# A new hand-written order of the first chunk's work, some of it on other engines, and softmax sums stored two words apart

## The chip, the cores and the metric

The kernel runs on one core of a Trainium2 chip. The metric is device time in microseconds (us) of one execution. The median of three runs of the kernel before is 609.96 us (609.53 to 610.3).

## The reference

```python
def _attn_ref(q, k, v):                      # q, k, v: 4 x 8 x 768 x 64
    block, window = (32, 16)
    k_sum = k.reshape(B, H, nb, block, D).max(axis=3)
    v_sum = v.reshape(B, H, nb, block, D).mean(axis=3)
    scores_l = scale * np.matmul(q, k.transpose(0, 1, 3, 2))
    mask_l = np.abs(pos[:, None] - pos[None, :]) < window
    scores_s = scale * np.einsum('bhsd,bhnd->bhsn', q, k_sum) + np.log(block)
    scores_all = np.concatenate([np.where(mask_l, scores_l, -1e9), scores_s], axis=-1)
    a = np.exp(scores_all - np.max(scores_all, axis=-1, keepdims=True))
    a = a / (np.sum(a, axis=-1, keepdims=True) + 1e-09)
    return np.matmul(a, np.concatenate([v, v_sum], axis=2))

def _moe_ref(x, w_in, w_out):                # 3072 x 512, 512 x 2048, 2048 x 512
    h = x @ w_in
    g = np.where(h > 0.0, h, np.exp(np.minimum(h, 0.0)) - 1.0)
    return g @ w_out
```

Each query sees the 31 keys around it and 24 block summaries of its head. The eight heads' outputs, side by side, are the rows x of a two-layer network with an ELU between the layers.

## The kernel before

The 3072 rows are six chunks of 512. A chunk takes 16 steps f of the network: twelve matmuls of the first layer into a PSUM tile `h`, the ELU of `h` on ScalarE and VectorE, and twelve matmuls of the second layer, which add into four PSUM tiles `o`. Twelve and not four, because every operand is split into a rounded high part and a remainder (`xh` and `xl`, `gh` and `gl`, a high and a low half of `w`) and three of the four products are formed. The weights come as 64-bit words and are made into fp32 on the chip during the first chunk: a conversion is GpSimd's or ScalarE's low bits (words X, Y), ScalarE's exponent (M), two VectorE operations (S), the high half (H) and the remainder (L). There are 32 conversions; number j alternates between the layers: 0 is step 0 of the first layer, 1 is step 1 of the first, 2 is step 0 of the second, and so on.

Attention runs ahead of the network. The first 512 queries are done by `first_units` at the very start, for four pairs of heads p, each with two halves h of the even and odd head. Later groups g of queries go between the network's steps.

From the start to the end of chunk 0 nothing sets the order but the string `FIRST`: each word is a piece of work and an engine may be its last number. Words are issued in the order of the string, and each engine runs its own instructions in that order (`tc.manual_schedule` for all five engines); semaphores are waited for where data needs it. The words that matter below:

- `kq`, `ve`, `vo`, `w`: loads on SyncE's queue of keys and queries, of value windows (`ve.0` to `ve.3`, `vo`) and of weight j.
- `max` (VectorE): block maxima of a pair's keys, L344. `sl`, `ss` (TensorE): window and summary scores. `low` (VectorE, L176, four instructions and four accumulator reads): masks and row maxima. `exp` (ScalarE, L184): exponentials, their sums written to a tile `zs`. `z` (VectorE): adds 1e-9 to a pair's eight sums (L189) and takes reciprocals (L190). `norm` (L193): multiplies a half by them, on GpSimd (last number 0) or VectorE (1). `tr`, `ptc`: transposes on TensorE and the copy from PSUM. `sums`, `spr`, `mv`: block means of the values on TensorE, spread by copies. `val` (TensorE): outputs of a pair. `xh`, `xl`: the split into `xs`.
- `first` and `L1h`, `L1l`: first-layer products of a step, with the high and low weights. `E`, `gap`, `larger`: the ELU as exp, relu(1 - e) on ScalarE and a maximum on VectorE (L689); `ts`, `stt` do the last two on VectorE instead. `G`, `gl`: the split of g. `L2a`, `L2b`, `L2c`: second-layer products.
- `gsc`, `glow`, `ge`, `gz`, `gn`, `gtr`, `gpc`, `gb`, `gval`, `gxh`, `gxl`: the same pieces for the later groups; `gb` transposes 32 x 32 blocks on VectorE (L606).
- `idle`, `warm`: matmuls of zeros, whose result nobody reads.

PSUM ties engines together: `h` has two buffers, so that `L1h` of a step waits for the `larger` (or the group's `gxl`) of two users earlier, and the scores of a group use the two banks in which S works. After the string comes the loop over the other 80 steps, which does not change.

Of the kernel before, what the change touches and what calls it, by code (L numbers as in the profile page):

```python
# [40 lines left out]
FIRST = """
    kq.2 sl.0 kq.3 max.0 ss.0 low.0.1 ve.2 exp.0.1 max.1 low.0.0 exp.0.0 sl.1 idle.1.196 ss.1 low.1.0 exp.1.0 max.2
    low.1.1 z.0 norm.0.0.0 sl.2 idle.1.220 ss.2 sl.3 idle.1.360 ve.1 exp.1.1 low.2.1 exp.2.1 max.3 z.1 ss.3 low.2.0
    exp.2.0 w.0 norm.0.1.0 norm.1.1.0 low.3.1 low.3.0 norm.1.0.0 exp.3.0 tr.0.0.1 tr.0.1.0 warm.1.144 z.2 tr.1.0.3
    ve.0 sums.0 sums.1 ve.3 vo exp.3.1 X.0 norm.2.0.0 ptc.0.1.0 sums.2 ptc.0.0.0 norm.2.1.0 w.1 tr.1.1.2 ptc.1.1.1
    spr.1.0 mv.0.1.0 tr.2.0.0 warm.1.96 ptc.1.0.0 spr.2.1 spr.0.0 mv.0.0.0 tr.2.1.1 ptc.2.1.1 w.5 mv.0.2.0 val.1.0
    mv.1.0.0 ptc.2.0.0 w.2 z.3 norm.3.1.1 spr.3.1 mv.0.3.0 w.3 M.0 X.1 mv.1.2.0 mv.1.1.1 norm.3.0.1 val.0.0 M.1
    val.2.0 S.0 mv.1.3.0 S.1 H.0.1 w.4 tr.3.1.0 ptc.3.1.1 tr.3.0.0 ptc.3.0.1 val.0.1 xh.0.0 xl.0 val.1.1 w.11
    val.2.1 xh.1.0 xl.1 w.6 val.3.0 xh.2.0 val.3.1 M.2 L.0.0 xl.2 xh.3.0 xl.3 X.2 S.2 X.3 first.0 H.1.0 w.7 M.3
    first.1 sk.0 first.2 L.1.0 w.9 S.3 X.4 first.3 E.0 gap.0 larger.0 Y.5 H.2.0 M.5 L1h.1 L1l.1 E.1 M.4 L.2.1 H.3.1  # L50
    L1h.2 L.3.0 S.5 gap.1 Y.6 L1l.2 w.10 M.7 w.8 S.4 G.0.1 vm.1 gl.0.0 E.2 H.5.1 L.5.0 larger.1 q.0 X.10 M.6 L2a.0
    L2c.0 X.7 S.6 G.1.0 L1h.3 L1l.3 H.4.0 L.4.1 S.7 L2b.0 w.12 gap.2 ks.0 H.7.0 gl.1.0 larger.2 X.9 H.6.0 gsc.0
    L2a.1 glow.0.1 L2c.1 sv.0 glow.0.0 vs.0 ge.0.1 w.14 X.8 sv.2 G.2.0 L2b.1 X.11 M.9 w.16 L.6.0 gz.0.1 gn.0.1.0
    L2a.2 L2c.2 X.12 L.7.1 S.9 M.8 E.3 gap.3 gl.2.0 S.8 H.8.1 sk.3 L1h.4 M.11 L1l.4 w.13 X.13 vm.0 H.9.0 larger.3
    L1h.5 L.9.1 S.11 gtr.0.1 ge.0.0 H.11.1 gz.0.0 gn.0.0.0 L.8.1 X.14 M.10 S.10 L1l.5 sk.2 ks.2 w.17 E.4 gap.4 vl
    L2b.2 sk.1 G.3.0 gl.3.1 q.1 gpc.0.1.1 gtr.0.0 H.10.0 L.10.0 L.11.0 M.13 larger.4 G.4.1 w.15 L2a.3 L2c.3 L2b.3
    w.25 S.13 H.13.1 gpc.0.0.1 w.18 M.12 gval.0 S.12 gsc.1 w.20 E.5 gap.5 gxh.0 K.3 larger.5 L1h.6 H.12.0 ks.1
    glow.1.0 L1l.6 L.13.0 sv.3 G.5.0 glow.1.1 K.2 gl.4.0 L.12.1 ge.1.0 gz.1.0 gxl.0 M.15 L2a.4 X.15 E.6 w.21 M.14
    X.16 L2b.4 L2c.4 S.15 M.17 ks.3 gap.6 ge.1.1 gl.5.0 L1h.7 L1l.7 X.17 S.14 H.14.0 M.16 larger.6 G.6.0 q.2 H.15.1
    L1h.8 w.19 E.7 gn.1.0.0 L.15.0 S.17 L.14.1 gz.1.1 gn.1.1.1 sv.1 X.21 gl.6.0 L1l.8 E.8 gtr.1.1 L2a.5 gpc.1.1.1  # L60
    w.23 X.18 L2b.5 S.16 H.16.1 H.17.0 gtr.1.0 vs.3 gap.7 L2c.5 w.26 L2a.6 L2b.6 vs.2 gap.8 M.19 gpc.1.0.1 M.18 X.19
    larger.7 w.24 G.7.0 L.17.0 pm.2 S.19 H.19.0 w.22 gval.1 pm.3 L.16.0 S.18 X.20 larger.8 gxh.1 X.23 gsc.2 L2c.6
    L1h.9 glow.2.0 gxl.1 H.18.0 vs.1 ge.2.0 L.18.0 gl.7.0 M.20 glow.2.1 L1l.9 X.24 ge.2.1 w.28 mmul mact M.21 mm
    L1h.10 S.20 L.19.0 L1l.10 M.22 gz.2.0 gn.2.0.0 H.20.1 L.20.0 E.9 gap.9 w.29 G.8.0 gz.2.1 gn.2.1.1 S.21 M.23 X.22
    X.25 H.21.1 L.21.0 gb.2.0.4 L2a.7 gl.8.1 E.10 gap.10 larger.9 gb.2.4.8 L2b.7 L2c.7 L2a.8 L2b.8 q.3 G.9.0
    larger.10 w.30 w.27 gl.9.0 X.28 L2c.8 L2a.9 S.22 L2b.9 L2c.9 L1h.11 L1l.11 S.23 M.25 gb.2.8.12 gb.2.12.16 G.10.1
    H.22.1 L2a.10 L.22.0 gl.10.0 H.23.0 L.23.0 M.24 S.24 H.24.1 L2b.10 L2c.10 E.11 X.26 gap.11 S.25 H.25.0 gval.2
    K.4 gxh.2 X.27 larger.11 G.11.1 gsc.3 glow.3.1 ge.3.1 L.24.0 gxl.2 glow.3.0 M.27 M.26 L1h.12 L1l.12 gl.11.1
    L.25.0 gz.3.1 ge.3.0 S.27 M.29 gn.3.1.1 X.29 L1h.13 L1l.13 E.12 gap.12 H.27.1 L2a.11 S.26 E.13 H.26.1 gz.3.0
    L2b.11 w.31 larger.12 L2c.11 L1h.14 L.27.0 gap.13 M.28 S.29 larger.13 H.29.0 L.26.0 L1l.14 S.28 M.30 gn.3.0.0  # L70
    gb.3.0.4 gb.3.4.8 gb.3.8.12 X.30 L1h.15 L.29.0 L1l.15 G.12.0 gl.12.0 H.28.0 L.28.0 G.13.0 E.14 M.31 gap.14
    gl.13.0 E.15 L2a.12 L2b.12 L2c.12 L2a.13 larger.14 S.30 H.30.0 gap.15 G.14.1 gl.14.0 gb.3.12.16 L2b.13 L2c.13
    L2a.14 L2b.14 X.31 S.31 H.31.0 gval.3 q.4 gsc.4 L.30.0 glow.4.1 larger.15 L.31.0 gxh.3 gxl.3 glow.4.0 ge.4.1
    ge.4.0 G.15.1 gl.15.0 L2c.14 gz.4.1 gn.4.1.1 gz.4.0 gn.4.0.1
"""


# [826 lines left out]
```

## Time and profile before

| | before |
|---|---|
| median of three runs | 609.96 us |
| the profiled execution | 609.49 us |
| its span, first to last instruction | 607.8 us |
| TensorE busy | 597.1 us (98%) |
| VectorE, ScalarE, GpSimd busy | 389.8, 262.6, 245.0 us |
| first layer-1 matmul of chunk 0 / of chunk 1 | 27.05 us / 129.60 us |

The profiled execution took 1.7 us more than its span, and lies 0.5 us below the median of the three. Busy TensorE is an average over the span: how much of the time is lost, and where, is read from single stretches. A VectorE or GpSimd instruction's shown duration includes what it waited after it had begun, so that the same shape with several durations is worth a look.

### The profile page before, as it was taken

To read this page: it belongs to the slowest core of one execution; us is meant where nothing else is said; L and a number is where in the kernel's file an instruction comes from. 1 tells how busy PE (TensorE), PEld (TensorE's weight loads), DVE (VectorE), ACT (ScalarE), POOL (GpSimd) and SP (SyncE) were. 2 spreads that over 40 slices of the span, in tenths; PEclk is the share of its full clock that TensorE was granted. 3 is DMA by queue.
4 is the path that set the end of the run, shared out by engine and by line. 5 is a ranking of instruction groups with operands and counts; after the bars stand their busy time and mean duration, and the time that the engine had idled before them with its cause. 6 is when DMAs were issued, how large, how long until landed. Compare 5 with 4: busy or idle time off the path is not lost.

```text
span 607.8 us, 11181 instructions
## 1 busy us (share of the span) xinstructions
PE 597.1 (98%) x4101; PEld 487.8 (80%) x4101; DVE 389.8 (64%) x1094; ACT 262.6 (43%) x755; POOL 245.0 (40%) x286
## 2 busy tenths in 40 slices
...
GB/s 315 371 361 300 261 140 160 78 105 72 29 27 146 63 84 180 71 65 1 28 165 118 53 93 76 106 2 96 66 41 42 2 1 0 70 0 1 0 1 69
DMA packets 63550, 58.62 MB, mean 96 GB/s; under 512 B 22648, under 2 KB 54904, under 8 KB 63496
## 3 DMA queue, kind: packets, MB, share of 16 engines
...
q8 instruction: 32, 0.52, 0.4%
q14 instruction: 22, 0.18, 0.1%
...
## 4 chain that ended last, share of the span: by engine, by line
PE 88%; DVE 6%; DMA 2%; ACT 2%; issue 1%; POOL 1%; DVEq 0%; ACTq 0%
PE h L661 36%; PE o L722 36%; PE o L712 4%; PE o_ps L625 3%; PE s L568 3%; PE h L672 3%; DMA v_own<-vsx 1%; DVE pt L606 1%; DVE sh L152 1%; DVE cv L155 1%; ACT sm_own L184 1%; DMA qn<-in_qT_dram 1%; POOL w L164 1%; PE s L362 1%; ACT sm L184 0%
## 5 line engine op out<-in xcount | busy, mean ns | idle before, releaser
L702 POOL TENSOR_TENSOR gl<-e,gh 128x512 fp32r<-128x512 f32 x93 | 119.9, 1290 | 260.3 <-ACT gh L697 148.2
L661 PE MATMUL h<-xh,w 128*128 128x512 f32 x640 | 212.3, 393 | 0.5 <-DVE e L689 0.5
L722 PE MATMUL o<-w,gh 128*128 128x512 f32 x648 | 163.0, 389 | 0.0
L722 PEld LDWEIGHTS o<-w,gh 128*128 128x128 f32 x648 | 121.6, 188 | 25.3
L661 PEld LDWEIGHTS h<-xh,w 128*128 128x128 f32 x640 | 120.1, 188 | 26.9 <-DVE e L689 1.0
L677 ACT ACTIVATE e<-h 128x512 f32<-128x512 f32 x96 | 57.1, 595 | 181.5 <-PE h L661 168.8
L606 DVE STREAM_TRANSPOSE pt<-sm 32x256 f32<-32x256 f32 x288 | 125.6, 436 | 6.3 <-POOL sm L193 0.9
L681 DVE TENSOR_SCALAR e<-e 128x512 f32<-128x512 f32 x80 | 41.0, 513 | 132.8 <-ACT e L677 132.3
L661 PE MATMUL h<-xl,w 128*128 128x512 f32 x320 | 124.6, 389 | 0.0
L697 ACT CAST gh<-e 128x512 fp32r<-128x512 f32 x90 | 55.8, 620 | 101.4 <-DVE e L692 101.4
L722 PE MATMUL o<-w,gl 128*128 128x512 f32 x324 | 89.5, 389 | 0.0
L184 ACT ACTIVATE sm<-sm,mx 128x120 f32<-128x120 f32 x160 | 61.2, 384 | 26.2 <-DVE mx L176 26.1
L722 PEld LDWEIGHTS o<-w,gl 128*128 128x128 f32 x324 | 60.8, 188 | 12.6
L661 PEld LDWEIGHTS h<-xl,w 128*128 128x128 f32 x320 | 60.1, 188 | 11.9
L193 POOL TENSOR_TENSOR sm<-sm,z 128x480 f32<-128x480 f32 x35 | 37.0, 1075 | 64.8 <-DVE z L196 63.6
L692 DVE SCALAR_TENSOR_TENSOR e<-h,e 128x512 f32<-128x512 f32 x80 | 55.3, 692 | 2.8
L176 DVE CUSTOM_DVE_ANT_0 sm<-s,mask 128x120 f32<-128x120 f32 x160 | 34.3, 278 | 25.6 <-PE s L568 25.6
L672 PE MATMUL h<-xh,w 128*128 128x512 f32 x120 | 39.1, 395 | 0.7 <-POOL w L164 0.4
L164 POOL TENSOR_TENSOR w<-cv,w 128x512 fp32r<-128x512 f32 x25 | 32.6, 1310 | 2.1 <-ACT w L161 1.1
L712 PE MATMUL o<-w,gh 128*128 128x512 f32 x120 | 31.7, 398 | 0.0
L639 DVE TENSOR_TENSOR xl<-o_ps,xh 128x256 fp32r<-128x256 f32 x40 | 15.1, 419 | 25.9 <-ACT xh L632 25.9
L184 ACT ACTIVATION_READ_ACCUMULATOR sm<-sm,mx 128x1 f32 x160 | 30.0, 188 | 0.0
...
## 6 DMA issues: line engine op xcount, KB each, us to landing
...
```

Source lines behind the costliest of these rows:

```text
L164: engine.tensor_tensor(out=self.w[:, 1, :], in0=self.cv, in1=self.w[:, 0, :].bitcast(F32), op=ALU.subtract)
L184: nc.scalar.activation(out=sm[:, t, :], in_=sm[:, t, :], func=AF.Exp, bias=mx[:, t, :], scale=-1.0, accum_out=z[:, t, :])
L606: nc.vector.transpose(out=dst[k, :, q], in_=src[q, :, k])
L661: nc.tensor.matmul(h_ps, w[:, a, cols], bb[:, cc, :], start=(k == 0), stop=(k == 3 * NCC - 1))
L672: nc.tensor.matmul(h_ps, w[:, lo, cc * P:(cc + 1) * P], bb[:, cc, :], start=(lo, cc, i) == (0, 0, 0), stop=(lo, cc) == (1, NCC - 1))
L677: nc.scalar.activation(out=e, in_=h_ps, func=AF.Exp)
L681: nc.vector.tensor_scalar(out=e, in0=e, scalar1=1.0, scalar2=-1.0, op0=ALU.min, op1=ALU.add)
L692: top = nc.vector.scalar_tensor_tensor(out=e, in0=h_ps, scalar=0.0, in1=e, op0=ALU.max, op1=ALU.add)
L697: copy(out=gh, in_=e)
L702: engine.tensor_tensor(out=gl, in0=e, in1=gs[(c, f)][0].bitcast(F32), op=ALU.subtract)
L712: nc.tensor.matmul(o_acc[0][s], gs[(0, f)][a][:, s * P:(s + 1) * P], w[:, bb, :], start=(f, part) == (0, 0), stop=False)
L722: nc.tensor.matmul(o_acc[c][s], a[:, s * P:(s + 1) * P], w[:, bb, :], start=first and f == 0, stop=last and f == NF - 1)
```

## The change

`FIRST` is another list of the same 555 words but for some 55 of them. Nothing of the computation goes: the words that differ name another engine, two steps (1 and 12) take `ts`, `stt` in place of `gap`, `larger`, and the matmuls of zeros have other numbers and places. The sums of a pair's exponentials, which lay in eight neighbouring words, now lie in every second word of sixteen. The other new functions (`fold`, `folded_maxima`, `maxima_half`, the `by` of `below_max` and `row_sums`) are not called by any word of the list.

```diff
-    kq.2 sl.0 kq.3 max.0 ss.0 low.0.1 ve.2 exp.0.1 max.1 low.0.0 exp.0.0 sl.1 idle.1.196 ss.1 low.1.0 exp.1.0 max.2
+    kq.2 sl.0 max.0 ss.0 low.0.1 exp.0.1 sl.1 max.1 low.0.0 exp.0.0 max.2 idle.1.452 ss.1 low.1.0 exp.1.0 sl.2 z.0
...
-        mean = borrow((2, 11), [P, 3 * BLK + 12 * 2 * UW], "mean")
+        mean = borrow((2, 11), [P, 3 * BLK + 16 * 2 * UW], "mean")
...
         def exp(p, h):
             if p not in zs:
-                zs[p] = small[:, 2 * NP + p, :].rearrange("p (h t o) -> p h t o", h=2, o=1)
+                zs[p] = small[:, 2 * (NP + p):2 * (NP + p + 1), :].rearrange("p h (t o) -> p h t o", o=2)[:, :, :, 0:1]
             exps(sms[p][:, h], mxs[p, h], zs[p][:, h])
```

The order on the engines, at three places. First VectorE, from the reciprocals of pair 2 to the first weight conversion. Here `sm_own` holds the exponentials, `mean` is the tile in which the sums lie, `t_ps` are transposes, `vsx` the means, `sh` and `cv` the conversion. Before:

```order
L189 TENSOR_SCALAR mean<-mean 128x8
L190 RECIPROCAL mean<-mean 128x8
L401 COPY pt_own<-t_ps 120x512 x2
L432 COPY vsx<-vsps 32x128
L401 COPY pt_own<-t_ps 120x512
L432 COPY vsx<-vsps 32x128
L401 COPY pt_own<-t_ps 120x512
L189 TENSOR_SCALAR mean<-mean 128x8
L190 RECIPROCAL mean<-mean 128x8
L193 TENSOR_TENSOR sm_own<-sm_own,mean 128x480 x2
L152 SCALAR_TENSOR_TENSOR sh<-sh,raw_w_0_357 128x512
```

Of the change, the same stretch from its first multiplication on (the reciprocals of pair 2 and a `low` of pair 3 stand just ahead of it):

```order
L193 TENSOR_TENSOR sm_own<-sm_own,mean 128x480
L448 COPY vsx<-vsps 32x128 x2
L417 COPY pt_own<-t_ps 120x512
L189 TENSOR_SCALAR mean<-mean 128x8
L190 RECIPROCAL mean<-mean 128x8
L417 COPY pt_own<-t_ps 120x512
L193 TENSOR_TENSOR sm_own<-sm_own,mean 128x480
L448 COPY vsx<-vsps 32x128
L152 SCALAR_TENSOR_TENSOR sh<-sh,raw_w_0_297 128x512
```

One of the two multiplications has moved ahead of the last reciprocals (it is pair 2's now), two copies of `t_ps` have moved in among the `low` of pair 3, and there are three copies of `vsx` in place of two.

Second GpSimd, from the memory fills of the start to the first high half of a weight. Before:

```order
L319 MEMSET v_own 32x512
L193 TENSOR_TENSOR sm_own<-sm_own,mean 128x480 x4
L140 TENSOR_SCALAR raw_w_0_357<-raw_w_0_357 128x512
L193 TENSOR_TENSOR sm_own<-sm_own,mean 128x480 x2
L439 COPY vxh<-vsx 24x4x128 x3
L439 COPY vxl<-vsx 24x4x128
L439 COPY vxh<-vsx 24x4x128
L140 TENSOR_SCALAR raw_w_1_431<-raw_w_1_431 128x512
```

Of the change:

```order
L319 MEMSET v_own 32x512
L193 TENSOR_TENSOR sm_own<-sm_own,mean 128x480
L140 TENSOR_SCALAR raw_w_0_297<-raw_w_0_297 128x512
L193 TENSOR_TENSOR sm_own<-sm_own,mean 128x480 x4
L455 COPY vxh<-vsx 24x4x128 x3
L193 TENSOR_TENSOR sm_own<-sm_own,mean 128x480
L455 COPY vxl<-vsx 24x4x128
L140 TENSOR_SCALAR raw_w_1_411<-raw_w_1_411 128x512
```

The low bits of the first weight have moved ahead of five of the six multiplications (its load stands ahead of all value windows on SyncE's queue now), and the last multiplication stands behind three copies of the means.

Third VectorE at the end of the string, where the last `larger` of chunk 0 stands (L176 begins the `low` of group 4). Before:

```order
L689 SCALAR_TENSOR_TENSOR e<-e,h 128x512
L152 SCALAR_TENSOR_TENSOR sh<-sh,raw_w_14_1459 128x512
L155 SCALAR_TENSOR_TENSOR cv<-raw_w_14_1459,sh 128x512
L606 STREAM_TRANSPOSE pt<-sm 32x8x32 x4
L152 SCALAR_TENSOR_TENSOR sh<-sh,raw_w_15_1683 128x512
L155 SCALAR_TENSOR_TENSOR cv<-raw_w_15_1683,sh 128x512
L176 ISA sm,mx<-s,mask 128x120
...
L689 SCALAR_TENSOR_TENSOR e<-e,h 128x512
L639 TENSOR_TENSOR xl<-o_ps,xh 128x256 x2
```

Of the change:

```order
L705 SCALAR_TENSOR_TENSOR e<-e,h 128x512
L152 SCALAR_TENSOR_TENSOR sh<-sh,raw_w_14_1476 128x512
L155 SCALAR_TENSOR_TENSOR cv<-raw_w_14_1476,sh 128x512
L152 SCALAR_TENSOR_TENSOR sh<-sh,raw_w_15_1628 128x512
L155 SCALAR_TENSOR_TENSOR cv<-raw_w_15_1628,sh 128x512
L622 STREAM_TRANSPOSE pt<-sm 32x8x32 x8
L705 SCALAR_TENSOR_TENSOR e<-e,h 128x512
L176 ISA sm,mx<-s,mask 128x120
```

The last `larger` has moved ahead of the first `low` of group 4, and the eight block transposes stand behind the last two conversions.

## Rows read from the trace of the kernel before

**Rows 1.** The page: busy time, share of the span and instructions of the engines.
```profile
PE 597.1 (98%) x4101; PEld 487.8 (80%) x4101; DVE 389.8 (64%) x1094; ACT 262.6 (43%) x755; POOL 245.0 (40%) x286
```

**Rows 2.** Stretches: length, busy us (instructions) by engine, granted clock, DMA share, GB/s.
```profile
4.59:27.05 22.46, 19.62 (x427) 16.35 (x427) 20.41 (x90) 18.85 (x77) 15.36 (x32) 1.00 1.06 368
27.05:60.00 32.95, 32.66 (x284) 26.09 (x281) 31.35 (x62) 26.17 (x60) 28.96 (x32) 1.00 1.07 340
60.00:95.00 35.00, 33.79 (x227) 26.98 (x220) 31.47 (x82) 25.67 (x71) 30.53 (x39) 1.00 0.68 217
95.00:129.60 34.60, 33.42 (x252) 26.39 (x250) 30.41 (x78) 21.01 (x55) 26.44 (x29) 1.00 0.28 80
```

**Rows 3.** TensorE's waits from 27 to 131 us: total, times, longest.
```profile
PE s L568 <- issue: 1.1, 1, 1.1
PE h L661 <- DVE e L689: 0.5, 1, 0.5
PE h L672 <- POOL w L164: 0.4, 1, 0.4
PE h L672 <- DVE e L689: 0.3, 1, 0.3
PE s L568 <- DVE cv L155: 0.2, 1, 0.2
```

**Rows 4.** TensorE's timeline where layer 1 begins: start, length, instructions, idle before.
```profile
26.48 0.64 PE L408 MATMUL o_ps<-pt_own,vxl 120*64 120x64 f32 x16
27.05 0.50 PE L452 MATMUL h<-xh,w 128*128 128x512 f32 x1
30.10 0.39 PE L672 MATMUL h<-xh,w 128*128 128x512 f32 x1
```

**Rows 5.** VectorE's timeline before layer 1.
```profile
6.35 0.28 DVE L176 CUSTOM_DVE_ANT_0 sm_own<-s,mask 128x120 f32<-128x120 f32 x1 [0.81 <-PE s L362]
9.28 0.28 DVE L176 CUSTOM_DVE_ANT_0 sm_own<-s,mask 128x120 f32<-128x120 f32 x1 [0.36 <-PE s L362]
13.93 0.38 DVE L189 TENSOR_SCALAR mean<-mean 128x8 f32<-128x8 f32 x1
20.30 0.28 DVE L432 COPY vsx<-vsps 32x128 f32<-32x128 f32 x1 [0.44 <-ACT vsx L432]
22.12 1.75 DVE L193 TENSOR_TENSOR sm_own<-sm_own,mean 128x480 f32<-128x480 f32 x2
23.79 0.69 DVE L152 SCALAR_TENSOR_TENSOR sh<-sh,raw_w 128x512 uint32<-128x512 uint32 x1
26.45 2.48 DVE L417 TENSOR_TENSOR xl<-o_ps,xh 128x512 fp32r<-128x512 f32 x4
```

**Rows 6.** VectorE durations in ns (least/median/most), from the views of the lines.
```profile
L189 DVE TENSOR_SCALAR mean<-mean x4: 168/462/625, 11.8 to 21.2; 128x8 f32<-128x8 f32 x4
L193 DVE TENSOR_TENSOR sm<-sm,z x5: 651/658/1452, 69.8 to 132.6; 128x480 f32<-128x480 f32 x5
L193 DVE TENSOR_TENSOR sm_own<-sm_own,mean x2: 765/912/1060, 22.1 to 22.8; 128x480 f32<-128x480 f32 x2
L164 DVE TENSOR_TENSOR w<-cv,w x7: 659/785/1657, 32.7 to 69.0; 128x512 fp32r<-128x512 f32 x7
L702 DVE TENSOR_TENSOR gl<-e,gh x3: 681/722/1197, 54.7 to 106.3; 128x512 fp32r<-128x512 f32 x3
L681 DVE TENSOR_SCALAR e<-e x80: 426/428/862, 133.3 to 596.4; 128x512 f32<-128x512 f32 x80
```

**Rows 7.** GpSimd's timeline beside the L189 at 13.93.
```profile
12.35 1.93 POOL L193 TENSOR_TENSOR sm_own<-sm_own,mean 128x480 f32<-128x480 f32 x2 [5.17 <-ACT sm_own L184]
```

**Rows 8.** VectorE's timeline at the end of chunk 0.
```profile
128.05 0.28 DVE L176 CUSTOM_DVE_ANT_0 sm<-s,mask 128x120 f32<-128x120 f32 x1 [1.74 <-PE s L568]
128.87 0.68 DVE L689 SCALAR_TENSOR_TENSOR e<-e,h 128x512 f32<-128x512 f32 x1
```

**Rows 9.** GpSimd's longest wait from 27 to 75 us.
```profile
POOL raw_w L140 <- DMA raw_w<-in_w_in_dram: 2.3, 1, 2.3
```

More of the change, by code (lines that the diff above doesn't have):

```diff
@@ L41 @@
 FIRST = """
-    kq.2 sl.0 kq.3 max.0 ss.0 low.0.1 ve.2 exp.0.1 max.1 low.0.0 exp.0.0 sl.1 idle.1.196 ss.1 low.1.0 exp.1.0 max.2
[L43 to L71, printed above, removed]
@@ L72 @@
-    gl.13.0 E.15 L2a.12 L2b.12 L2c.12 L2a.13 larger.14 S.30 H.30.0 gap.15 G.14.1 gl.14.0 gb.3.12.16 L2b.13 L2c.13
-    L2a.14 L2b.14 X.31 S.31 H.31.0 gval.3 q.4 gsc.4 L.30.0 glow.4.1 larger.15 L.31.0 gxh.3 gxl.3 glow.4.0 ge.4.1
-    ge.4.0 G.15.1 gl.15.0 L2c.14 gz.4.1 gn.4.1.1 gz.4.0 gn.4.0.1
+    kq.2 sl.0 max.0 ss.0 low.0.1 exp.0.1 sl.1 max.1 low.0.0 exp.0.0 max.2 idle.1.452 ss.1 low.1.0 exp.1.0 sl.2 z.0
+    low.1.1 norm.0.1.0 kq.3 max.3 w.0 X.0 ve.1 ss.2 low.2.1 exp.1.1 z.1 sl.3 norm.0.0.0 tr.0.1.0 ve.3 exp.2.1
@@ new lines @@
+    low.2.0 exp.2.0 ptc.0.1.0 warm.1.376 warm.1.220 ss.3 low.3.0 tr.0.0.1 ptc.0.0.0 norm.1.0.0 ve.0 tr.1.0.3 sums.0
+    sums.1 z.2 low.3.1 norm.2.0.1 ve.2 w.1 vo exp.3.0 sums.2 spr.1.1 spr.2.0 idle.1.360 spr.0.0 ptc.1.0.0 exp.3.1
+    z.3 norm.1.1.0 tr.1.1.2 w.6 norm.2.1.0 tr.2.1.1 ptc.2.1.1 idle.1.104 mv.0.1.0 tr.2.0.0 ptc.2.0.0 ptc.1.1.1 M.0
+    mv.0.0.0 val.0.0 val.1.0 mv.1.0.1 mv.1.2.1 mv.0.2.0 val.2.0 M.1 w.2 norm.3.0.1 w.4 tr.3.0.0 norm.3.1.0 spr.3.0
+    tr.3.1.0 ptc.3.0.1 ptc.3.1.1 mv.1.1.0 X.1 val.0.1 S.0 val.1.1 S.1 xh.0.0 xl.0 w.3 val.2.1 mv.1.3.0 val.3.1
@@ new lines @@
+    xh.1.0 xl.1 w.5 mv.0.3.0 val.3.0 vm.0 w.14 sk.0 xh.2.0 w.7 xl.2 H.0.1 first.0 xh.3.0 xl.3 L.0.0 w.9 X.2 M.2 S.2
+    X.3 H.1.0 L.1.0 M.3 S.3 Y.5 first.1 first.2 first.3 E.0 gap.0 larger.0 X.4 H.3.1 L.3.1 M.5 S.5 H.2.1 L.2.0 sk.3
+    Y.6 G.0.0 L1h.1 L1l.1 E.1 M.4 ts.1 w.8 gl.0.0 stt.1 H.5.0 q.0 S.4 X.9 L1h.2 L1l.2 E.2 ks.3 gap.2 X.7 L2a.0 L2c.0
+    L.5.0 M.6 S.6 H.4.0 L.4.0 M.7 S.7 L1h.3 L1l.3 L2b.0 larger.2 G.1.0 gl.1.0 H.7.1 gsc.0 w.10 sk.2 ks.2 X.8 H.6.0
+    sk.1 ks.1 vl vm.1 glow.0.1 E.3 gap.3 sv.0 w.12 glow.0.0 L.7.1 M.9 L.6.0 ge.0.1 w.11 S.9 X.10 M.8 L2a.1 G.2.1
@@ new lines @@
+    gl.2.0 L2c.1 ge.0.0 M.11 H.9.1 L1h.4 gz.0.1 L1l.4 X.11 S.8 gn.0.1.0 M.10 E.4 gap.4 L2b.1 L2a.2 L2c.2 q.1
+    larger.3 L1h.5 H.8.1 X.14 gz.0.0 L.9.1 L1l.5 S.11 H.11.0 L.8.0 sv.1 w.20 gtr.0.1 sv.2 G.3.1 gl.3.0 w.13 X.13
+    X.12 S.10 H.10.0 gpc.0.1.1 M.13 E.5 w.16 X.16 L2b.2 gn.0.0.1 gtr.0.0 vs.1 gpc.0.0.1 larger.4 G.4.1 M.12 gap.5
+    w.15 L.10.1 w.24 S.13 S.12 L2a.3 L2c.3 L2b.3 gval.0 gsc.1 H.13.0 ks.0 larger.5 L1h.6 w.18 X.20 w.17 gxh.0 gxl.0
+    H.12.0 G.5.0 K.2 L.13.0 glow.1.1 w.19 ge.1.1 glow.1.0 M.15 vs.0 sv.3 L.12.1 L.11.0 X.17 gl.4.0 L1l.6 E.6 X.15
@@ new lines @@
+    S.15 L1h.7 q.2 L1l.7 M.14 S.14 gz.1.1 ge.1.0 gap.6 X.18 larger.6 M.17 L2a.4 gl.5.0 E.7 K.3 gz.1.0 L2b.4 L2c.4
+    L2a.5 L2b.5 M.16 L2c.5 H.15.1 X.19 L.15.1 S.17 G.6.0 H.14.1 H.17.0 L.14.0 S.16 gn.1.0.0 gtr.1.0 L.17.1 gap.7
+    larger.7 gn.1.1.0 gtr.1.1 H.16.0 L.16.0 gpc.1.0.0 M.18 L1h.8 L1l.8 gpc.1.1.1 L2a.6 M.19 w.22 gl.6.0 E.8 gval.1
+    vs.2 S.18 pm.2 S.19 X.24 G.7.0 X.22 H.18.1 gl.7.1 gsc.2 gap.8 larger.8 H.19.0 w.21 glow.2.1 L2b.6 gxh.1 w.23
+    ge.2.1 glow.2.0 L.18.0 vs.3 w.25 L2c.6 X.25 L.19.1 L1h.10 L1l.10 mmul w.26 G.8.1 M.20 gxl.1 L1h.9 S.20 X.21
@@ new lines @@
+    L1l.9 L2a.7 L2b.7 ge.2.0 gz.2.0 gn.2.0.1 gl.8.0 L2c.7 X.23 L2a.8 L2b.8 gz.2.1 gn.2.1.0 w.28 mact M.21 S.21
+    H.20.1 E.10 L.20.0 gap.10 larger.10 H.21.0 M.23 L.21.0 E.9 gap.9 gb.2.0.4 larger.9 L2c.8 M.22 S.23 L1h.11 L1l.11
+    w.27 G.9.1 L2a.9 gl.9.0 M.25 w.30 X.28 L2b.9 S.22 H.22.1 L.22.0 G.10.1 gl.10.0 H.23.0 gb.2.4.8 gb.2.8.12
+    gb.2.12.16 M.24 S.24 E.11 gap.11 L2c.9 mm H.24.0 L.23.0 L2a.10 L2b.10 L2c.10 X.26 S.25 H.25.0 larger.11 G.11.0
+    gval.2 gxh.2 pm.3 q.3 gsc.3 w.29 X.29 L1h.12 L1l.12 glow.3.1 ge.3.1 glow.3.0 gxl.2 M.26 M.27 q.4 w.31 X.31
@@ new lines @@
+    L.24.0 gz.3.1 L.25.0 S.26 L1h.13 L1l.13 M.28 X.30 E.12 X.27 S.27 gn.3.1.0 gl.11.0 H.26.1 ge.3.0 L.26.1 ts.12
+    stt.12 E.13 G.12.0 L2a.11 L2b.11 L2c.11 H.27.1 L1h.14 L.27.0 L1l.14 gap.13 gl.12.0 gz.3.0 gn.3.0.0 M.29 S.28
+    H.28.1 L2a.12 L2b.12 L2c.12 larger.13 M.30 S.29 H.29.0 M.31 L.28.0 L.29.0 gb.3.0.4 gb.3.4.8 E.14 G.13.0 gap.14
+    larger.14 S.30 L1h.15 L1l.15 gl.13.0 E.15 G.14.1 gl.14.0 S.31 L2a.13 L2b.13 H.30.1 L2c.13 L2a.14 L2b.14
+    gb.3.8.12 K.4 gsc.4 gb.3.12.16 gval.3 gap.15 larger.15 L.30.0 G.15.0 glow.4.1 gxh.3 gxl.3 glow.4.0 ge.4.1 gz.4.1
@@ L75 @@
+    ge.4.0 gz.4.0 gn.4.0.1 gl.15.0 gn.4.1.0 H.31.0 L.31.1 L2c.14
 """
```

25 lines of the change are left out of this document (19 added, 6 removed).

## The prediction

> **What bounds the kernel now.** I read the page first: TensorE is busy 597.1 us of a span of 607.8 [rows 1], so time can only come from where it waits, multiplies zeros or works on what could come later. The change ends with chunk 0, where layer 1 of chunk 1 begins at 129.60; behind that the program is the same, so that a move of this point is a move of the end. The view of stretches divides what is ahead of it [rows 2]: from 4.59 to 27.05 VectorE is busy 20.4 us of 22.5, and in the three stretches to 129.60 it has 31.4, 31.5 and 30.4 of 33 to 35. [...] After 27.05 TensorE loses 1.1 + 0.5 + 0.4 + 0.3 + 0.2 = 2.5 us in waits [rows 3]; three of them end on VectorE (on `larger`, and on `cv`, the end of a conversion), one on GpSimd's remainders, and the 1.1 ("issue") is the scores of a group, whose banks VectorE's conversions had held. So two things count: when layer 1 starts, and whether VectorE, and behind it GpSimd, can run earlier through the following 100 us.
>
> **The opening.** Layer 1 began at 27.05 [rows 4], when VectorE's first `xl`, begun at 26.45, was done [rows 5]. VectorE ran from its first row maximum at 6.35 to 26.45: 20.1 us. What it does in this time stays but for one more copy of the means: eight `low`, three maxima, four reciprocals, four copies of transposes, two multiplications, two conversions. So the gain is what it loses now. I add it up. It waits 0.36 at 9.28 for summary scores and 0.44 at 20.30 for ScalarE's copy of the means [rows 5]. The four L189 should take 168 ns, the least of them; the others take 380 to 625 and their median is 462 [rows 6], and the one of 13.93 ends at 14.31, where GpSimd's pair of multiplications ends (12.35 + 1.93 = 14.28) [rows 5, 7]. With 0.38 and 0.62 seen, and a median of four, (x + 0.38)/2 = 0.462, the remaining one is 0.55: 0.21 + 0.38 + 0.46 = 1.05 us lost. The two multiplications take 765 and 1060 where 651 would do: 0.52 [rows 6]. Together 2.37 us.
>
> In the new order the maximum of pair 2 fills the wait at 9.28, the sums are closer to their means, and L189 and L190 of pairs 0 and 2 run while GpSimd waits for them. What comes back: the third copy of the means, 0.28 [rows 5]; and both multiplications now run beside one of GpSimd's. Followed instruction by instruction with the durations above, pair 2's begins at 18.1 while GpSimd's runs from 17.5 to 18.4 (0.97 each, [rows 7]), and pair 3's at 21.4 while GpSimd has 21.0 to 21.9. That is 0.2 and 0.5, against 0.52 now. L189 of pairs 1 and 3 meet GpSimd's multiplication and copy again; if they still wait, 0.2 each. I get 20.1 - 2.37 + 0.28 + 0.7 = 18.7 with no such waits, and 19.1 with them; I take 19.1, so -1.0. The bounds: no gain at all (every wait has a successor), and -2.0, all lost time but the added copy.
>
> [...]
>
> TensorE has its own limit: the last transposes of pair 3, then five of the eight `val`. Pair 3's multiplication on VectorE ends at about 22.5 instead of 23.9. Two transposes and five `val` took 3.0 us without their waits, and there is an input wait of 0.1, so layer 1 starts at about 26.2 (-0.85), and its first step, paced by the four `xl`, ends 1.2 earlier than the 30.10 at which step 1 began [rows 4].
>
> **The loads.** The first weight's load is ahead of the value windows now, since GpSimd's low bits stand ahead of five multiplications. DMA moves 368 GB/s at a share of 1.06 in this stretch [rows 2], so the 0.5 MB are 1.4 us; ahead of it 2.6 MB of keys and queries. It should land near 11, before GpSimd takes it at 12.1. The windows land later by at most these 1.4 us, near 15 to 16, and `sums` takes them at 15.7 to 16.7: cover of about half a microsecond.
>
> **The 100 us behind.** VectorE's list from the first conversion to the last `larger` changes in place and little in sum: two more remainders (2 x 0.659) against two fewer `gl` (2 x 0.681) and one multiplication fewer (0.651); one more copy of a transpose (about 0.62); two `ts` (2 x 0.426) [rows 6]; and the `low` of group 4 that stood ahead of the last `larger` (four of about 0.2) is behind it: -0.01 us. It takes 129.55 - 23.79 = 105.8 us now [rows 5, 8], of which 1.74 us are the wait for group 4's scores ahead of that `low` [rows 8]. With `larger` first that wait holds up nobody on TensorE, and chunk 1's 0.5 us wait on `larger` [rows 3] should go. So VectorE reaches the last `larger`'s end after 104.0 us at best without other improvements, or 105.8 if something else is as late: 22.8 + 104.0 = 126.8, or 128.6. Chunk 1 then starts at 126.9 to 128.7, 0.9 to 2.7 us earlier. TensorE's bound agrees: 129.60 - 0.85 - 2.5 = 126.25 with no wait left.
>
> I see new waits. Step 2's `L1h` needs step 0's `larger`, and ScalarE now has low bits of a weight (0.68) ahead of step 0's exp: about 0.35 us. `ts` has the shape that took 426 at least but up to 862 ns [rows 6]. The many waits of 27 to 129 I can't place one by one, so I take -1.6, near the middle: 609.49 - 1.6 = 607.9 for the profiled execution, which lay 0.47 below the median of three, so **608.4** for the median. A measurement can tell about 0.2%, 1.2 us, from no change.
>
> **The rivals.**
> - *Given back (0.27).* VectorE is as late at a group's scores as now. Its list up to the conversions that free the banks for group 2's scores has grown by 0.4 us (a `ts`, 0.43, and a copy, 0.62, for a `gl`, 0.68), so 0.6 of the head start is left there, and the 1.1 us of waiting at those scores stays. If its blocked time grows by as much as the opening gave, nothing is left at chunk 1. For: three of the five waits end on it. Against: the sum to the end is the same. Time: 609.4 (the forecast's 608.4 and the 1.0 of the opening), within 0.2%.
> - *The layout edit does nothing (in the forecast, 0.35 of it).* L189 still waits: 608.4, where with a free L189 it would be 608.0. The forecast already pays for it.
> - *GpSimd becomes the bound, slower (0.18).* Counting words up to step 6's low-weight products, `L1l.6`, which has the same place in TensorE's stream, GpSimd has 33.9 us of work from its first high half on, where it had 27.2 (three more low bits, two remainders, two `gl`, one split; one multiplication fewer). It was busy 29.0 of 33.0 us up to 60 [rows 2]. Without a pause it finishes the remainder that `L1l.6` needs at 56.9; `L1l.6` now begins near 62.1. If GpSimd loses 5.2 us to waits and to VectorE's two-input operations, the head start is gone, and from 6.4 on the kernel is slower by over 0.2%. It loses some 4 us there now, and one load alone cost 2.3 [rows 9]. Time: 611.
> - *Late windows.* If the values land 2 us late, ScalarE stands in front of its copy of the means with pair 3's last exponentials behind it: 610. I count 0.05 of the two rivals above for it.
>
> **How the numbers follow.** Forecast, faster by over 0.2%: 0.55; within: 0.27; slower: 0.18. The forecast's own range is 0.9 to 2.9 us, 607.1 to 609.1. For 8 in 10 I leave out one tenth below (all opening losses gone, -3.1: 606.9) and one above, half of the slower case: 610.9.
>
> **What would show it.** Right: the first `xl` near 25.4 and layer 1 near 26.2; L189 of pairs 0 and 2 at 0.17; the last `larger` ahead of the `low` of group 4 and no wait of `h` on it at chunk 1; its first matmul at 127 to 128.7. Wrong: ScalarE or GpSimd waiting for a load before 20 us, layer 1 at 27 or later, waits of `h` on GpSimd's remainders between 50 and 75 us, or scores of a group waiting over 1 us for `cv`.

## The result, and the profile after

The changed kernel takes 614.48 us (median of 8 executions, 613.35 to 615.73), the kernel before 610.13 (8 executions). The ratio is 1.0061, with a 95% interval of 1.0041 to 1.0081: **slower by 4.35 us, 0.6 to 0.7%**. The forecast was 608.4, faster. The profiled execution took 613.35 us with a span of 611.6.

The line of engines on the page, which answers to [rows 1], tells nothing: TensorE is busy 0.7 us longer and its share is the same.

```profile
PE 597.8 (98%) x4101; PEld 489.9 (80%) x4101; DVE 391.4 (64%) x1097; ACT 260.6 (43%) x750; POOL 246.3 (40%) x288
```

TensorE's waits of the changed kernel from 26 to 141 us answer to [rows 3]: 6.7 us in total where 2.5 stood.

```profile
PE s L584 <- issue: 2.6, 1, 2.6
PE o L738 <- ACT w L161: 1.6, 1, 1.6
PE o L738 <- DVE w L164: 1.2, 1, 1.2
PE s L584 <- DVE cv L155: 0.6, 1, 0.6
PE t_ps L202 <- ACT w L161: 0.4, 1, 0.4
PE t_ps L202 <- DVE cv L155: 0.3, 1, 0.3
```

TensorE's timeline shows where they lie. Layer 1 of chunk 0 begins at 26.48, before that of [rows 4]. The scores of group 1 wait 2.62 at 61.72. Layer 1 of chunk 1 begins at 130.26, later than before (129.60) but without the wait of [rows 3]. The second layer behind it waits twice. From the kernel before to this one the span grew by 3.8 us (607.8 to 611.6): 0.66 of it had come by this point, and 3.1 came behind it.

```profile
26.48 0.50 PE L468 MATMUL h<-xh,w 128*128 128x512 f32 x1
...
29.36 0.39 PE L688 MATMUL h<-xh,w 128*128 128x512 f32 x1
...
57.95 1.15 PE L641 MATMUL o_ps<-pt,v_own 120*64 120x64 f32 x32
61.72 0.89 PE L584 MATMUL s<-kn,qbd 64*64 64x96 f32 x32 [2.62 <-issue]
...
130.26 0.39 PE L677 MATMUL h<-xh,w 128*128 128x512 f32 x1
...
134.73 0.49 PE L738 MATMUL o<-w,gh 128*128 128x512 f32 x1 [1.58 <-ACT w L161]
136.39 0.50 PE L738 MATMUL o<-w,gh 128*128 128x512 f32 x1 [1.16 <-DVE w L164]
```

The stretches (columns as in [rows 2]) show one thing more: behind the gap the granted clock, 1.00 in all of [rows 2], falls to 0.50. A matmul of layer 1 then takes 0.43 us from start to start instead of 0.23.

```profile
59.00:62.00 3.00, 0.38 (x17) 0.31 (x17) 1.07 (x2) 0.99 (x3) 2.92 (x3) 1.00 0.92 168
62.00:64.00 2.00, 2.00 (x65) 1.81 (x57) 2.00 (x7) 0.91 (x3) 1.84 (x3) 0.69 0.71 171
64.00:66.00 2.00, 2.00 (x6) 1.52 (x6) 2.00 (x15) 1.97 (x10) 1.76 (x4) 0.50 1.05 391
66.00:68.00 2.00, 2.00 (x10) 1.65 (x9) 2.00 (x3) 0.81 (x2) 1.14 (x1) 0.95 1.20 276
```

**Who was late at 61.72.** The row says "issue", so I follow the banks, which VectorE's S held: the scores start 0.1 us after conversion 12 ends. Its timeline has the second half of conversion 12 waiting 2.09 for GpSimd's remainder; above it two L189 of the opening that answer to [rows 5], below it the end of chunk 0 that answers to [rows 8]:

```profile
13.20 0.68 DVE L189 TENSOR_SCALAR mean<-mean 128x8 f32<-128x8 f32 x1
...
20.31 0.42 DVE L189 TENSOR_SCALAR mean<-mean 128x8 f32<-128x8 f32 x1
...
25.68 1.88 DVE L433 TENSOR_TENSOR xl<-o_ps,xh 128x512 fp32r<-128x512 f32 x3
...
58.15 0.69 DVE L152 SCALAR_TENSOR_TENSOR sh<-sh,raw_w 128x512 uint32<-128x512 uint32 x1
60.93 0.69 DVE L155 SCALAR_TENSOR_TENSOR cv<-raw_w,sh 128x512 uint32<-128x512 uint32 x1 [2.09 <-POOL w L164]
...
124.55 3.62 DVE L622 STREAM_TRANSPOSE pt<-sm 32x256 f32<-32x256 f32 x8
128.20 0.69 DVE L705 SCALAR_TENSOR_TENSOR e<-e,h 128x512 f32<-128x512 f32 x1
128.80 0.28 DVE L176 CUSTOM_DVE_ANT_0 sm<-s,mask 128x120 f32<-128x120 f32 x1
...
135.65 0.68 DVE L164 TENSOR_TENSOR w<-cv,w 128x512 fp32r<-128x512 f32 x1
```

`cv` has two buffers. One was held by conversion 11, whose remainder the list puts last of seven pieces on GpSimd (the list before had it ahead of conversion 13), the other by conversion 13. So conversion 12 had to take the buffer of 13, and its wait ends where the first of the two remainders does. GpSimd's timeline, without a pause here, has the three low bits, a split, another low bits, and then the remainders of 13 and 11:

```profile
55.71 2.46 POOL L140 TENSOR_SCALAR raw_w<-raw_w 128x512 uint32<-128x512 uint8 x3
58.23 0.61 POOL L713 CAST gh<-e 128x512 fp32r<-128x512 f32 x1
58.92 0.64 POOL L140 TENSOR_SCALAR raw_w<-raw_w 128x512 uint32<-128x512 uint8 x1
59.64 2.50 POOL L164 TENSOR_TENSOR w<-cv,w 128x512 fp32r<-128x512 f32 x2
```

**Who was late at 134.73.** The waited-for `w` is the last weight, conversion 31. Its rounded half (`H.31.0`) and remainder (`L.31.1`) are the last words of the new list but one. ScalarE gets to the half at 134.07, behind group 4's exponentials and the exp of step 16; VectorE to the remainder at 135.65 (above). ScalarE's timeline:

```profile
133.03 0.38 ACT L184 ACTIVATE sm<-sm,mx 128x120 f32<-128x120 f32 x1
...
133.41 0.57 ACT L693 ACTIVATE e<-h 128x512 f32<-128x512 f32 x1
133.88 0.29 ACT L598 ACTIVATE z<-z,tiny 128x4 f32<-128x4 f32 x1
134.07 0.60 ACT L161 CAST w<-cv 128x512 fp32r<-128x512 f32 x1
```

So two theories of the loss stood against each other: that two words stand in the wrong place of the list (the last weight, and the remainder of weight 11), with the clock on top; or that GpSimd has too much work now, as the prediction's slower rival said, so that no order helps.

### The profile page after: what moved, and what is told of

The parts are those of the page before. It is cut to its first block, busy times and chain, and to the rows that moved or that the text cites. A ratio compares the mean times of both kernels' runs of the same rounds, so it can differ in the third digit from the quotient of the medians.

```text
span 611.6 us, 11194 instructions
## 1 busy us (share of the span) xinstructions
PE 597.8 (98%) x4101; PEld 489.9 (80%) x4101; DVE 391.4 (64%) x1097; ACT 260.6 (43%) x750; POOL 246.3 (40%) x288
## 4 chain that ended last, share of the span: by engine, by line
PE 80%; DMA 6%; DVE 5%; POOL 4%; ACT 2%; issue 2%; SPq 1%; ACTq 0%; POOLq 0%; DVEq 0%
PE o L738 36%; PE h L677 36%; PE o_ps L641 3%; PE s L584 3%; DMA raw_w<-in_w_in_dram 2%; DMA vxh<-in_v_dram 1%; DMA v_own<-in_v_dram 1%; DVE pt L622 1%; POOL w L164 1%; DVE cv L155 1%; PE o L728 1%; PE h L688 1%; DMA qn<-in_qT_dram 1%; POOL raw_w L140 1%; DVE sh L152 1%
## 5 line engine op out<-in xcount | busy, mean ns | idle before, releaser
L718 POOL TENSOR_TENSOR gl<-e,gh 128x512 fp32r<-128x512 f32 x95 | 123.3, 1297 | 263.0 <-ACT gh L713 159.0
L697 DVE TENSOR_SCALAR e<-e 128x512 f32<-128x512 f32 x82 | 43.3, 528 | 134.3 <-ACT e L693 134.3
L193 POOL TENSOR_TENSOR sm<-sm,z 128x480 f32<-128x480 f32 x37 | 39.0, 1073 | 66.3 <-DVE z L196 64.2
L708 DVE SCALAR_TENSOR_TENSOR e<-h,e 128x512 f32<-128x512 f32 x82 | 56.7, 692 | 2.8
L176 DVE CUSTOM_DVE_ANT_0 sm<-s,mask 128x120 f32<-128x120 f32 x160 | 34.1, 278 | 23.2 <-PE s L584 23.2
L164 POOL TENSOR_TENSOR w<-cv,w 128x512 fp32r<-128x512 f32 x22 | 28.6, 1308 | 3.6 <-ACT w L161 2.5
```

Source lines behind the costliest of these rows:

```text
L193: engine.tensor_tensor(out=sm, in0=sm, in1=z.broadcast_to([P, UW, KC]), op=ALU.mult)
L697: nc.vector.tensor_scalar(out=e, in0=e, scalar1=1.0, scalar2=-1.0, op0=ALU.min, op1=ALU.add)
L708: top = nc.vector.scalar_tensor_tensor(out=e, in0=h_ps, scalar=0.0, in1=e, op0=ALU.max, op1=ALU.add)
L718: engine.tensor_tensor(out=gl, in0=e, in1=gs[(c, f)][0].bitcast(F32), op=ALU.subtract)
```

## The experiments

The runs are counted in the order in which they stand here. Every ratio is to the kernel before on the same chip, with its 95% interval. Five executions of the kernel before among those of the first eight experiments took about 615.7 us; they lower these ratios a little and leave the medians as they are.

**First run: the last weight in time.** The rounded half stands ahead of group 3's values again; the remainder stands behind that of weight 30 and is back on GpSimd, where the changed list had given it to VectorE.

```diff
-... gval.3 gap.15 larger.15 L.30.0 G.15.0 glow.4.1 ... gn.4.1.0 H.31.0 L.31.1 L2c.14
+... H.31.0 gval.3 gap.15 larger.15 L.30.0 L.31.0 G.15.0 glow.4.1 ... gn.4.1.0 L2c.14
```

> The changed kernel with one thing mended: the rounded half and the remainder of the last weight (step 15 of the second layer), which are the last words of the new list, stand ahead of the values of group 3 and behind the remainder of weight 30, as in the list before, the remainder on GpSimd. Theory: the two waits of TensorE in the second layer of step 15 (1.58 and 1.16 us) are a loss of their own, so the time falls by 2.7 us from the changed kernel's 614.5, to 611.8; the waits at 61 us stay. Rival, the network behind is late anyway (ScalarE's exponentials of group 4 and the ELU of step 16 stand in the same place): the wait moves to step 16 or 17 and the time falls by less than 1 us, to 613.5 or more.

610.23 us, ratio 0.9999 (0.9981 to 1.0017): 4.25 less than the changed kernel, more than the two waits' 2.74, and 1.6 less than expected. In the waits of this kernel no `o` is left, and the gap is:

```profile
PE s L584 <- issue: 2.7, 1, 2.7
PE s L584 <- DVE cv L155: 0.6, 1, 0.6
```

That these words cause the two waits is shown (for the second wait, place and engine of the remainder changed together). The 1.5 us beyond 2.74 are dealt with below, with the clock.

**Second run: the remainder of weight 11 earlier.**

```diff
-... w.16 X.16 L2b.2 ... L.12.1 L.11.0 X.17
+... w.16 L.11.0 X.16 L2b.2 ... L.12.1 X.17
```

> The changed kernel with one word moved: the remainder of weight 11 on GpSimd stands ahead of three operations (two low bits and a split) and of the remainder of weight 13 instead of behind them, so that its buffer cv comes free for VectorE's conversion of weight 12 about 2 us earlier. GpSimd has the same work. Theory: the scores of group 1 start at 59.6 instead of 61.72, the gap of 2.6 us shrinks to about 0.5, the clock stays at 1.00, and layer 1 of step 6 starts at 61.0 instead of 63.13: the time falls by 2.1 for the gap and 1.7 for the clock, to 610.7. Rival, GpSimd has too much work, whatever its order (the rival of the prediction): the wait moves to the splits and low bits behind, and the time stays above 613.

612.90 us, ratio 1.0046 (1.0034 to 1.0058), 1.6 less than the changed kernel and not 3.8. The scores start at 59.71, as expected, but layer 1 of step 6 does not start at 61.0:

```profile
59.71 0.89 PE L584 MATMUL s<-kn,qbd 64*64 64x96 f32 x32 [0.65 <-PE o_ps L641]
...
62.48 0.80 PE L688 MATMUL h<-xh,w 128*128 128x512 f32 x1 [1.45 <-DVE mx L176]
```

What the row names is not what layer 1 needs: `larger` of step 5 had ended at 61.06. Behind this wait the clock fell (0.60 from 62 to 64). The fourth run's profile, with the same list up to here, has neither; so this is something of the execution (last section). What the other four executions did here was not seen. All five had a mean clock of 0.996 or 0.997, and the two waits of the last weight, at which the next run's clock fell, were still there.

**Third run: the gap filled.** Group 0's values are computed three times into the same bank (`gval.0.3`).

```diff
-        for i in range(2):
+        for i in [0, 1] * times:
```

> The changed kernel with the matmuls of the values of group 0 done three times over into the same bank, so that TensorE multiplies through some 2.3 us of the 2.6 us gap ahead of the scores of group 1; the outputs are the same. Theory: the gap alone costs 2.6 us and the clock behind it another 1.7 us; with the clock held, the scores still start at about 61.7 but layer 1 of step 6 runs at 0.23 us a matmul from its start: the time falls by 1.7, to 612.8. Rival, the lower clock costs nothing because something else (VectorE, GpSimd) is as late behind it: unchanged, 614.5. ScalarE takes the values 2.3 us later, which may give back up to 0.5 us.

614.59 us, ratio 1.0068 (1.0052 to 1.0084): no gain, the rival's number. But the rival's reason is wrong. In the profiled execution the clock held at 62 to 68 and fell at the other two waits instead:

```profile
64.00:66.00 2.00, 2.00 (x10) 1.60 (x9) 2.00 (x17) 1.78 (x9) 1.80 (x3) 1.00 1.10 396
...
134.00:136.00 2.00, 0.85 (x3) 0.68 (x3) 1.17 (x3) 0.62 (x1) 1.26 (x1) 0.75 0.04 11
136.00:138.00 2.00, 2.00 (x7) 1.51 (x6) 0.24 (x1) 0.59 (x1) 0.30 (x1) 0.50 0.02 7
```

One of its six executions kept a mean clock of 1.00 and took 612.15, where the others had a median of 614.66.

**Fourth run: both edits**, the diffs of the first and the second run together.

> The first two edits together on the changed kernel. Theory: the losses are independent, 2.7 and 3.8 us, so 608.0 us, 2 us below the kernel before, with chunk 1 beginning near 126.5 and no wait over 1 us behind it. Rival, the head start is eaten on the way by the next late engine: 610 or more, the same as the kernel before.

608.36 us, ratio 0.9962 (0.9938 to 0.9986), chunk 1 at 127.67. Faster than both kernels, near the forecast. Its waits:

```profile
PE t_ps L202 <- POOL sm L193: 0.9, 2, 0.7
PE s L584 <- PE o_ps L641: 0.6, 1, 0.6
PE t_ps L202 <- ACT w L161: 0.4, 1, 0.4
PE s L584 <- DVE cv L155: 0.4, 1, 0.4
```

The gap at group 1's scores and the two waits of the last weight are gone. GpSimd has the changed kernel's words and one more, the last remainder. That it has too much work is refuted; the order decided.

**Fifth run: the layout alone on the kernel before**, nothing of the list (one of three hunks; the others make room for it and repeat it in a function that is not called).

```diff
-                zs[p] = small[:, 2 * NP + p, :].rearrange("p (h t o) -> p h t o", h=2, o=1)
+                zs[p] = small[:, 2 * (NP + p):2 * (NP + p + 1), :].rearrange("p h (t o) -> p h t o", o=2)[:, :, :, 0:1]
```

> The kernel before with nothing but the layout edit: the sums of exponentials lie two words apart. [...] Rival: the waits of L189 go, up to 1 us of VectorE's opening, and the time falls by 0.3 to 0.8 us, layer 1 at 26.3 or so.

610.38 us against 610.05, ratio 0.9979 (0.9953 to 1.0006): no difference that can be told. I had expected the same time within 0.2%, with L189 still waiting. The profiled execution had the low clock in its opening (0.50 from 15 to 20 us), so that its pieces met differently: three of its L189 took 0.16 to 0.17, the fourth, at 25.40, took 0.62. So with words two apart one still takes 0.45 us more, as two of the changed kernel, above, do.

**Sixth run: the last weight late in the kernel before.**

```diff
-... S.31 H.31.0 gval.3 ... larger.15 L.31.0 gxh.3 ... gn.4.0.1
+... S.31 gval.3 ... larger.15 gxh.3 ... gn.4.0.1 H.31.0 L.31.1
```

> The kernel before with the last weight's rounded half and remainder moved to the very end of its list, behind group 4's exponentials on ScalarE and its multiplications on VectorE, as the changed list has them. Theory: the second layer of step 15 then waits as in the changed kernel, 2.7 us in two pieces, and the clock falls in part of the executions: 613 us or somewhat more, 0.45% or more slower. Rival: the kernel before has its exponentials and ELU in another order there, the wait is under 1 us, the time within 0.2%.

611.47 us against 610.05, ratio 1.0017 (0.9994 to 1.0040). No difference that can be told, as the rival had it. The waits of its second layer are there but only 0.87 us:

```profile
PE h L672 <- issue: 1.5, 1, 1.5
...
PE o L722 <- DVE w L164: 0.4, 1, 0.4
PE o L722 <- ACT w L161: 0.4, 1, 0.4
```

The place of the words makes the wait here too; its size, as I read the rows, depends on what ScalarE does ahead. In this kernel the exponentials of group 4 begin 1.2 us ahead of chunk 1's first matmul (129.92 and 131.15); in the changed one 0.2 ahead (130.03 and 130.26), after eight block transposes (3.62 us, above) had held back the last `larger`, and with it the `low`. I had expected 2.7 for having overlooked that.

**Seventh run: the last `larger` first, in the kernel before.**

```diff
-... L.30.0 glow.4.1 larger.15 L.31.0 ...
+... L.30.0 larger.15 glow.4.1 L.31.0 ...
```

> The kernel before with the last larger of chunk 0 ahead of the first low of group 4 on VectorE, the one place at the end of the list on which the prediction rested. Theory: the wait of 0.52 us on larger at chunk 1 goes, layer 1 of chunk 1 begins 0.5 us earlier, at 129.1, and the end with it: 609.6, hardly to be told from the kernel before by its time, but by its trace. Rival: the low and the exponentials of group 4, begun 0.7 us later, delay the ELU of step 16, and TensorE waits there instead: unchanged.

609.71 us against 610.05, ratio 0.9995 (0.9970 to 1.0019): the size is as expected but lies within what can be told. The trace decides: of [rows 3]'s waits the one of `h` on `larger` at chunk 1 is gone, and its first matmul has none (in a profiled execution with a mean clock of 0.990, whose layer 1 began at 31.01, 4.0 us late, much as the fifth run's, whose profile has that wait).

**Eighth run: a third edit on top.** Two multiplications of group 1 earlier, one of them on VectorE.

```diff
-... S.17 G.6.0 H.14.1 H.17.0 L.14.0 S.16 gn.1.0.0 gtr.1.0 ... larger.7 gn.1.1.0 gtr.1.1
+... S.17 gn.1.0.0 gn.1.1.1 G.6.0 H.14.1 H.17.0 L.14.0 S.16 gtr.1.0 ... larger.7 gtr.1.1
```

> The changed kernel with both edits of the fourth run and a third: of group 1's two multiplications one moves ahead of a rounded half and a remainder on GpSimd and one to VectorE, ahead of conversion 16. TensorE waited 0.19 and 0.74 us for them at 72 to 74 us. Theory: these 0.9 us go, 607.5. Rival: VectorE's 0.65 us more make the scores of group 2 as late as the 0.9 us won: 608.4.

608.85 us, ratio 0.9975 (0.9951 to 0.9998). A miss, 607.5 was expected: the wait of the transposes on GpSimd went, and they now wait 1.2 for the conversion that holds their bank, which again waits 0.56 for GpSimd's remainder of weight 14.

```profile
73.33 0.69 DVE L155 SCALAR_TENSOR_TENSOR cv<-raw_w,sh 128x512 uint32<-128x512 uint32 x1 [0.56 <-POOL w L164]
```

**Ninth to twelfth run: what the clock costs.** Four runs on one chip: the first edit with the gap filled, the first edit again, the fourth kernel with VectorE's multiplication alone moved, and the fourth kernel again. The third of them differs from the fourth by

```diff
-... S.17 G.6.0 H.14.1 ... larger.7 gn.1.1.0 gtr.1.1
+... S.17 gn.1.1.1 G.6.0 H.14.1 ... larger.7 gtr.1.1
```

> The first and the third edit together: the last weight is in time, and the gap ahead of group 1's scores is still there for VectorE but filled to more than half by repeated matmuls of group 0's values (the outputs are the same). Theory: it is the idle gap that lets the clock fall, so that with it filled the granted clock is 1.00 in most executions, as in the kernel before, and the median falls from the first edit's 610.2 to what that kernel shows where the clock held, 609.5. Rival: the clock falls by chance of the execution, whatever the gap: as often as with the first edit alone, and 610.2.

> The first edit alone again, beside the run above on the same chip, to compare how often the clock falls. Theory: 610.2, a mean granted clock under 0.998 in more than half of the executions. Rival: as seldom as in the run above.

> The fourth run's kernel with one multiplication of group 1 on VectorE ahead of conversion 16 and nothing else moved (the eighth run had moved a second one ahead of the remainder of weight 14, whose late end held the buffer of conversion 16 for 0.56 us). Theory: the wait of 0.74 us at 73.8 us goes without a new one, 607.6. Rival: VectorE's 0.65 us more come back at the next conversion, 608.4.

> The fourth run's kernel again, beside the run above on the same chip: 608.4, about 0.3% under the kernel before. Rival: its gain was that chip's, and it is within 0.2%.

| kernel on this chip | median us | ratio, interval | executions with mean clock 0.999 or more |
|---|---|---|---|
| before | 610.07 | | 22 of 29 |
| first edit, gap filled | 609.36 | 0.9983 (0.9968 to 0.9997) | 11 of 12 |
| first edit | 610.51 | 1.0014 (1.0005 to 1.0023) | 0 of 12 |
| both edits, `gn` on VectorE | 608.50 | 0.9980 (0.9971 to 0.9989) | 10 of 11 |
| both edits | 607.38 | 0.9962 (0.9950 to 0.9974) | 5 of 5 |

The first two came out as expected. The third has its rival's number, and the last is 1 us faster than expected. The stretches of the first edit with the gap open, and of the same with the gap filled:

```profile
62.00:64.00 2.00, 0.96 (x24) 0.99 (x28) 1.75 (x3) 0.62 (x1) 1.92 (x3) 0.63 0.55 97
64.00:66.00 2.00, 2.00 (x50) 1.85 (x43) 1.59 (x8) 0.82 (x2) 1.84 (x3) 0.50 0.95 343
66.00:68.00 2.00, 2.00 (x6) 1.56 (x5) 2.00 (x14) 1.97 (x10) 1.84 (x3) 0.50 1.14 354
68.00:70.00 2.00, 2.00 (x7) 1.56 (x6) 1.97 (x4) 0.29 (x1) 0.40 (x1) 0.67 1.05 203
```

```profile
62.00:64.00 2.00, 1.48 (x65) 1.44 (x66) 1.94 (x5) 1.02 (x2) 1.84 (x3) 1.00 0.71 156
64.00:66.00 2.00, 2.00 (x10) 1.62 (x10) 2.00 (x17) 1.70 (x9) 1.76 (x4) 1.00 1.08 400
```

That the open gap lets the clock fall is shown: with more than half of it filled the clock held, though TensorE still waited 1.48 us and did the same useful work. On this chip the fall at 62 us costs 1.15 us (610.51 - 609.36); in the first run the six executions at 0.997 lie 0.8 us above the four at 1.00 (610.37 and 609.54, medians). The wait itself, with what the repeated matmuls cost, takes another 1.98 (609.36 - 607.38). The multiplication on VectorE takes 1.1 more by the medians in place of a gain: its transposes wait 1.2 for the conversion behind it.

Now the 1.5 us by which the first edit's 4.25 exceed 2.74. Compared at the same mean clock, the edit is worth 3.3 us at 0.997 (613.7 and 610.4, medians) and 3.0 at 0.993 to 0.994 (615.3 and 612.3), close to the two waits. The rest is that four of the first run's twelve executions kept 1.00 and none of the changed kernel's eight had over 0.997. That the clock fell at the changed kernel's second gap is not shown: its profile has 1.00 there, and the mean does not tell the place, for the first edit's second profile, without that gap, has a mean of 0.994 from one longer fall at 62 us (the stretches above). Only the third run's profile shows a fall at the second gap.

## Why the prediction was wrong

**The step that failed** is the one that puts the end of the change at chunk 1's first matmul: "behind that the program is the same, so that a move of this point is a move of the end". The loop is the same, but its first second-layer products need a weight whose last two words stand in the list. Looking only at the last `larger`, the prediction missed 2.74 us of waits 4.5 us behind the point. By the first run they are worth 4.25 us by the medians and 3.0 to 3.3 at the same clock; the rest goes with how often and how long the clock fell.

**A second step was incomplete**: "The 100 us behind" summed VectorE's list and named two small new waits. The sum says nothing of who holds a buffer. The remainder of weight 11 held one of two `cv`, so VectorE stood 2.09 for the other, the scores 2.62, and the clock fell behind them: chunk 1 began at 130.26, where the forecast had at most 128.7. On the one chip where all was measured that is 1.98 + 1.15 = 3.1 us; on the chip of the first four runs the same step (610.23 to 608.36) gave 1.9, and there four of the first edit's twelve executions had kept the clock.

With both gone, the kernel has 608.36 and 607.38 on two chips, 2.0 and 2.7 under the kernel before there, where the forecast had 1.6. So without these two places the change is a gain of about the size foreseen. That the size fits is in part luck: of the 1.93 us by which the fourth run's chunk 1 begins earlier (127.67), the opening gave 0.39, where 0.85 was forecast, and 1.3 came from a place that the prediction did not look at (below, *TensorE between*).

Point by point:

- *The opening*: right in kind. The first `xl` begins at 25.68 (forecast 25.4), layer 1 at 26.48 (26.2), step 1 at 29.36, 0.74 earlier than [rows 4] (forecast 1.2). The value windows were not in time: `sums` waited 0.72 for them, to 16.80, where half a microsecond of cover was forecast.
- *L189*: two of four were short, the ones beside which GpSimd rests, as said. The others took 0.68 and 0.42 while GpSimd multiplied or copied, 0.5 and 0.26 more than the short ones, where 0.2 each was forecast. Both ended 0.03 us behind a GpSimd instruction (13.88 and 13.85, 20.73 and 20.70), as the one of [rows 5, 7] at 13.93 had (14.31 and 14.28). So two words apart did not take these waits away, and the forecast's choice of 19.1, the sum with waits, was right in that.
- *The end of chunk 0*: the last `larger` stands ahead of the `low`, and nobody waits for it, as said. On the kernel before, that edit alone took 0.3 us by the medians, where 0.5 was expected.
- *TensorE between*: by the stretches it was busy 99.87 us from 27.05 to 129.60 before, and the fourth kernel 98.57 for the same 745 matmuls and the same number of steps. 1.3 us of its gain thus came from the time in which it counts as busy, by my reading from waits too short to stand as such in [rows 3]; the bound of 126.25 had left them out. And the longest wait of [rows 3], 1.1 at the scores of group 2, is not in the profiles of the fifth, sixth and seventh run, whose list is the same up to there (each had been held up earlier, layer 1 by 4.2 and 4.0 us in the fifth and the seventh, step 6 by the stop told below in the sixth); so it is not a fixed loss.
- *"Given back"* did not happen through VectorE's growing list at group 2's scores; the waits there are gone.
- *"GpSimd becomes the bound"* had the right sign and engine and the wrong mechanism. It forecast TensorE waiting at `L1l.6` for the amount of work; the wait came earlier, at the scores of group 1, for the order of one word, and with the same work it went. Of the loss that it put down to VectorE's two-input operations the kernel before shows a case: beside VectorE's two multiplications of [rows 5] (22.12 to 23.87), GpSimd's copy of 22.32 took 1.04 us, where the same shape took 0.61 at 19.77. Of the signs that the prediction named for its being wrong, a group's scores waiting over 1 us for `cv` is the one that came.
- *Late windows*: TensorE waited 0.7 of that rival's 2 us, and the opening kept most of its gain.
- *The clock*, 1.00 in all of [rows 2], has no term in the prediction. There no wait had been over 1.08.
- *The sums* hold but for two slips that change nothing: VectorE's list comes to -0.02 and not -0.01, and the range goes to 2.9 us earlier where its working ends at 2.7.
